# A layer-normalized attention and mixer kernel: the first chunk's q and k made in two halves, and the second chunk turned behind the values

## The chip, the cores and the metric

The kernel runs on one core of one Trainium2 chip. The metric is the device time of one execution in microseconds, taken as the median of several runs. A core has TensorE (PE in the profile; PEld is its weight load), VectorE (DVE), ScalarE (ACT), GpSimd (POOL) and SyncE (SP, which here issues the DMAs). Each engine works through a queue of its own.

## The reference

Cut to what matters, for 2048 rows of 512 numbers:

```python
xn = layernorm(x)                              # over the 512 columns
q, k, v = xn @ wqkv                            # 32 heads of 16 columns
scores = q k^T / 4, row i sees columns i-255 .. i
s = softmax(scores) v @ wo
y = layernorm(xn)
g = silu(gelu(y @ w1 + b1) @ w2 + b2)          # 512 -> 1792 -> 512
out = x + s * g
```

All of it is float32. The kernel reaches that precision with float32r products in three passes: each operand is split into a high part (a cast to float32r) and a low part (the rest), and high times high, high times low and low times high are added up.

## The kernel before

**Chunks and tiles.** The rows are worked on in four chunks of 512 rows, each of four tiles of 128 rows. A chunk is loaded (`xs[c]`), normalized in place, turned by PE (16 transposes of 128x128, four for each of the four 128-column parts `kt`) and split into `big[:, 0, kt]` (high, a cast by ACT) and `big[:, 1, kt]` (low, a subtraction by DVE from the PSUM bank). In the profile `big` is called xnT. Then come its q, k (`job_qk(n, c)`, twelve products of 512 columns, for a group `n` of heads) and its values (`job_v(hf, i)`, 24 products of 256 columns for a pair of 128-row blocks; the tile is pv, or vt after the copy to SBUF).

**Normalization.** `layernorm` (L87) returns the steps of each tile. Either DVE takes the mean and variance (`each`: bn, mvs, ve), POOL takes the power -1/2 (rss), DVE makes the shift, and ACT or DVE applies it (`end`); or, for the tiles named in `by_sums`, ACT takes the sum (`total`), POOL the mean (nm), ACT the squares (`squares`), POOL ve and rss, and `end_sums` the rest. `n_act` is the number of tiles that ACT applies.

**The first chunk.** L762 to L775: for each of the four tiles statistics, normalization and `transpose0`, which writes 128 columns of each of four PSUM tiles `tr0[kt]` (two are called tr in the profile, two fb; each is one bank of 512 columns). Two extra products of `ident` follow the first two tiles. Then ACT casts the weights of q, k (wqb from wqkr), POOL makes their low part, DVE casts the weights of the values (wva from wvr), POOL makes their low part, and L790 splits the four banks, a whole bank at a time.

**The order of the work.** Except for SyncE ahead of L756, a wrapper (`Ordered`) keeps the instructions of each engine in the order of the code. The main loop (L906) runs over slots `t` from -16 on, each of two halves, `fill_in(t, 0)` and `fill_in(t, 1)`. `group(c)` (L795) is a list of jobs that `spread` (L525) lays evenly over eight half slots; for `c = 0` these are slots -16 to -13. At the end of each slot stands `run(lns.get(t))`, further steps of the normalization:

```python
lns = {-16: [ln1[1][1], ln1[0][2], invert3, ln1[2][1], ln1[1][2], ln1[3][1]], -15: [ln2[1][0], ones],
       -14: [ln2[0][0], ln2[2][0], ln2[0][1], ln2[3][0]], -13: [ln2[i][-1] for i in range(4)],
```

`ln1`, `ln2`, `ln3` are the steps of chunks 1, 2, 3; `ones` is a POOL memset of a column of vt. Before, `job_x(1)` (the 16 transposes of chunk 1, each followed in the fourth by ACT's cast and DVE's subtraction) is issued in slot -14, between the two halves of the values `job_v(0, 1)`. Its first three `kt` use the tiles fb0, fb1 and the first bank of zo. `job_qk(0, 1)` in slot -12 writes fb0. The product of `job_qk(0, 0)` lies in the first bank of xy; its high part (sh) is copied by ACT in slot -16, its low part (pjr) is made by DVE in slot -15, and both are sent by DMA to `slots[0]` (qk), from which the first scores, `max_block(0, m)`, are made at the end of slot -12 and later.

**Waits.** The kernel is written in a tile framework: it says which tile each instruction reads and writes, and the framework places the semaphore waits between engines. Where the kernel wants more of them, it adds them by hand (`add_manual_dep`).

Of the kernel before, what the change touches and what calls it, by code (L numbers as in the profile page):

```python
# [9 lines left out]
F32 = mybir.dt.float32  # L10
# [3 lines left out]
ALU = mybir.AluOpType  # L14
# [36 lines left out]
def mixer_kernel(ctx, tc, x, wqk, wv, wo, w1, b1, w2, b2, out):  # L51
# [32 lines left out]
    rss = small.tile([P, 8 * NCH], F32, tag="rs", name="rss", bufs=1)  # L84
    squared = set()

    def layernorm(ts, c, n_act=4, by_sums=(), end_act=False, apart=()):  # L87

        n = len(ts)
        nm = small.tile([P, n], F32, tag="nm", name=f"nm{c}") if by_sums else None  # L90
        sh = small.tile([P, n], F32, tag="shift", name=f"shift{c}")
        mv, sm, rs = mvs[:, n * c: n * c + n], sums[:, n * c: n * c + n], rss[:, n * c: n * c + n]
        squared.update(n * c + i for i in by_sums)

        def total(i):

            nc.scalar.activation(x23[:, 8], ts[i], AF.Identity, accum_out=sm[:, i, 0:1])
            nc.gpsimd.tensor_scalar(nm[:, i: i + 1], sm[:, i, 0:1], -1.0 / D, None, op0=ALU.mult)

        def squares(i):  # L100

            nc.scalar.activation(x23[:, 8], ts[i], AF.Square, bias=nm[:, i: i + 1], accum_out=sm[:, i, 1:2])
            ve = small.tile([P, 1], F32, tag="ve1", name=f"ve{c}_{i}")
            nc.gpsimd.tensor_scalar(ve, sm[:, i, 1:2], 1.0 / D, EPS, op0=ALU.mult, op1=ALU.add)
            nc.gpsimd.tensor_tensor(rs[:, i: i + 1], ve, mhalf[:, :1], op=ALU.pow)

        def end_sums(i):
            if end_act:
                nc.vector.tensor_mul(sh[:, i: i + 1], nm[:, i: i + 1], rs[:, i: i + 1])
                apply(i, True)  # L110
                return
            nc.gpsimd.tensor_scalar(ts[i], ts[i], nm[:, i: i + 1], rs[:, i: i + 1], op0=ALU.add, op1=ALU.mult)

        def each(i):

            st = small.tile([P, 6], F32, tag="bn", name=f"bn{c}_{i}")
            nc.vector.bn_stats(st, ts[i])
            nc.vector.bn_aggr(mv[:, i], st)
            ve = small.tile([P, 1], F32, tag="ve1", name=f"ve{c}_{i}")
            nc.vector.tensor_scalar(ve, mv[:, i, 1:2], EPS, None, op0=ALU.add)  # L120
            if i in apart:
                return lambda: power(i, ve)
            power(i, ve)

        def power(i, ve):
            nc.gpsimd.tensor_tensor(rs[:, i: i + 1], ve, mhalf[:, :1], op=ALU.pow)

        def apply(i, on_act):
            if on_act:
                nc.scalar.activation(ts[i], ts[i], AF.Identity, bias=sh[:, i: i + 1], scale=rs[:, i: i + 1])  # L130
            else:
                nc.vector.tensor_scalar(ts[i], ts[i], mv[:, i, 0:1], rs[:, i: i + 1],
                                        op0=ALU.subtract, op1=ALU.mult)

        def end(i):

            if i < n_act:
                nc.vector.scalar_tensor_tensor(sh[:, i: i + 1], mv[:, i, 0:1], -1.0, rs[:, i: i + 1],
                                               op0=ALU.mult, op1=ALU.mult)
            apply(i, i < n_act)  # L140
        return [(lambda i=i: total(i), lambda i=i: squares(i), lambda i=i: end_sums(i)) if i in by_sums else
                (lambda i=i: each(i), lambda i=i: end(i)) for i in range(n)]

    def run(steps):
        for step in steps:
            step()
# [149 lines left out]
    def job_qk(n, c):  # L296

        box = []
        ops = [(kt, a, b) for kt in range(KT) for a, b in PASSES]
        if not n:  # L300
            ops.sort(key=lambda o: o[2])
        sl = slice(512 * c, 512 * (c + 1))

        def mm(i):
            if i == 0:
                box.append(fill_bank() if c else xy[:, 0])
            kt, a, b = ops[i]
            nc.tensor.matmul(box[0], wqs[n][:, a, kt], big[:, b, kt, sl],
                             start=(i == 0), stop=(i == len(ops) - 1))

        def half(bank, j, i, r, **flags):
            kt, a, b = ops[i]
            return nc.tensor.matmul(bank[:, 0:256], wqs[n][r, a, kt],
                                    big[r, b, kt, 512 * c + 256 * j: 512 * c + 256 * (j + 1)], **flags)

        def send(src, qk, tt):
            copy_rows(slots[n % 2][tt:P:4, qk, :, sl], src[64 * qk: 64 * qk + 64])

        def finish():
            hi = sgp.tile([P, 512], F32R, tag="sh", name=f"sh_{n}_{c}", bufs=2)  # L320
            raw = t2.tile([P, 512], F32, tag="t2", name=f"pjr_{n}_{c}")
            lo = raw.bitcast(F32R)
            if n or c > 1:
                for j, bank in enumerate(box):
                    nc.scalar.copy(raw[:, 256 * j: 256 * (j + 1)], bank[:, 0:256])
                box[:] = [raw]
            wide = 512 // len(box)
            parts = [(bank[:, 0:wide], slice(wide * j, wide * (j + 1))) for j, bank in enumerate(box)]

            def high():  # L330
                for src, at_ in parts:
                    nc.scalar.copy(hi[:, at_], src)
                behind(now[0], send_high)

            def send_high():
                for qk, tt in ((1, 0), (0, 0), (1, 2), (0, 1)):
                    send(hi, qk, tt)

            def low():
                for src, at_ in parts:  # L340
                    (nc.gpsimd if n or c > 1 else nc.vector).tensor_tensor(lo[:, at_], src, hi[:, at_].bitcast(F32),
                                                                  op=ALU.subtract)
                behind(now[0], send_low)

            def send_low():
                send(lo, 1, 1)
                send(lo, 0, 2)

            later(1 if n else 0, high)
            later(3 if n else 1, low)  # L350
        if n or c > 1:
            return half, finish, box
        return [(216, mm, i) for i in range(len(ops))], finish

    def by_halves(job, banks, first, second, seer=None):
# [23 lines left out]
    def job_v(hf, i):  # L379
# [3 lines left out]
        def mm(k):  # L383
            if k == 0:
                box.append(ps_st.tile([P, 2, 256], F32, tag="b", name=f"pv_{hf}_{i}"))
            j, kt, (a, b) = k // 12, k % 12 // 3, PASSES[k % 3]
            kb = 2 * i + j
            nc.tensor.matmul(box[0][:, j], big[:, a, kt, P * kb: P * (kb + 1)], wva[:, b, kt],
                             start=(k % 12 == 0), stop=(k % 12 == 11))
# [372 lines left out]
    def transpose0(i):  # L762
        for kt in range(KT):
            nc.tensor.transpose(tr0[kt][:, P * i: P * (i + 1)], xs[0][i][:, P * kt: P * (kt + 1)], ident)
        for _ in range(2 if i < 2 else 0):
            nc.tensor.matmul(zo[:, 0, 0:P], ident, ident, start=True, stop=True)

    ln = layernorm(xs[0], 0, 3)
    for i in range(4):
        ln[i][0]()  # L770
        if i:
            ln[i - 1][1]()
            transpose0(i - 1)
    ln[3][1]()
    transpose0(3)  # L775
    split_wqk(0)
    ln1 = layernorm(xs[1], 1, 2, by_sums=(0, 1), end_act=True, apart=(3,))
    ln2 = layernorm(xs[2], 2, by_sums=(0,))
    ln3 = layernorm(xs[3], 3, by_sums=range(4))
    n, raw = raws["qk"]  # L780
    nc.gpsimd.tensor_tensor(wqs[0][:, 1], raw, wqs[0][:, 0].bitcast(F32), op=ALU.subtract)
    for j, raw in enumerate(raws["v"]):
        nc.vector.tensor_copy(wva[:, 0, 2 * j: 2 * j + 2], raw)
        nc.gpsimd.tensor_tensor(wva[:, 1, 2 * j: 2 * j + 2], raw, wva[:, 0, 2 * j: 2 * j + 2].bitcast(F32),
                                op=ALU.subtract)
        if j == 0:
            ln1[0][0]()
    nc.gpsimd.affine_select(out=upper, in_=upper, pattern=[[1, P]], compare_op=ALU.is_gt,
                            fill=0.0, base=0, channel_multiplier=-1)
    for kt in range(KT):  # L790
        split(big[:, 0, kt, 0:512], big[:, 1, kt, 0:512], tr0[kt])
    run([ln1[0][1], ln1[1][0], ln1[2][0]])
    invert3 = ln1[3][0]()

    def group(c):  # L795
        if c == 0:
            (ops, finish), (x_ops, _) = job_v(0, 1), job_x(1)
            return [job_qk(0, 0), job_v(0, 0), (ops[:12] + x_ops, lambda: None), (ops[12:], finish)]
        return [job_qk(0, c), job_v(0, 2 * c), job_x(c + 1), job_v(0, 2 * c + 1)]
    for c in range(2):  # L800
        fills.update(spread(group(c), [(4 * c - 16 + i // 2, i % 2) for i in range(8)]))
# [620 lines left out]
```

## Time and profile before

| | |
|---|---|
| median of 3 runs | 733.74 us (733.71 to 734.0) |
| profiled execution | 733.78 us |
| its span in the trace | 732.0 us |
| PE busy | 719.5 us (98%) |
| DVE, ACT, POOL busy | 496.5, 427.7, 321.6 us |
| first product of `job_qk(0, 0)` | 10.76 us from the span's start |
| end of `job_qk(0, 1)` | 24.42 us |

The page of a profile gives busy time by engine over the whole span, and a line of 40 slices. For a change in the first 25 us it is read together with the timeline (each row: start, duration, engine, line, operation, tile written, tile read, shape, count, and in brackets the idle time of the engine just before and what ended it), with the chain that ended last (start, duration, what) and with the table of busy time by stretch. Nearly all instructions carry line L43, that of a helper, so tiles tell them apart. Times are in us from the start of the span.

### The profile page before, as it was taken

Reading aid. Unit: us, or ns where it says so; the run is one execution under the profiler, and the core shown is the slowest. Engines: PE = TensorE matmul, PEld = TensorE weight load, DVE = VectorE, ACT = ScalarE, POOL = GpSimd, SP = SyncE. Lnnn points to the kernel's source line nnn. Section 1 sums busy time; section 2 is a strip of 40 time slices with the busy share of each in tenths; the row PEclk is TensorE's granted clock in tenths of the full one; section 3 lists DMA queues with packets and bytes.
Section 4 is the critical chain, followed back from the end, with each engine's and each line's share of the span. In section 5 each row is a group of like instructions: output and inputs, shape, how many; then the busy total and the mean of one; then the engine's idle time right before and its main releaser. Section 6 shows DMA issues by size and latency. Waiting matters only on the chain.

```text
span 732.0 us, 19063 instructions
## 1 busy us (share of the span) xinstructions
PE 719.5 (98%) x7584; PEld 586.1 (80%) x7584; DVE 496.5 (68%) x735; ACT 427.7 (58%) x724; POOL 321.6 (44%) x678
## 2 busy tenths in 40 slices
PE   8999999999999999999999999999999999999997
PEld 7997777777778887777776788888888888888886
DVE  6887776877766777777882657446687855667823
ACT  7767777877777676888878735232343734541001
POOL 7344767767677665777877540203302000001102
PEclk9999999999999999999999999999999999999999
DMA  8324356777776733667624367347223312253701
GB/s 294 81 48 105 89 137 171 215 229 217 207 197 184 211 119 98 169 160 203 182 79 160 119 230 200 145 130 244 87 57 116 115 59 87 65 189 110 252 19 58
DMA packets 61528, 106.77 MB, mean 146 GB/s; under 512 B 12096, under 2 KB 12352, under 8 KB 61440
## 3 DMA queue, kind: packets, MB, share of 16 engines
q1 hardware_dynamic: 61440, 105.56, 49.3%
q8 instruction: 60, 0.98, 0.6%
q14 instruction: 28, 0.23, 0.1%
HBM read 54.53 MB, written 33.82 MB: 121 GB/s over the span
## 4 chain that ended last, share of the span: by engine, by line
PE 92%; ACT 3%; DVE 2%; DMA 1%; issue 1%; POOL 0%; SPq 0%; DVEq 0%; ACTq 0%; POOLq 0%
PE acc L43 20%; PE fb L43 20%; PE zo L43 13%; PE stb L43 9%; PE p L43 9%; PE s L43 6%; PE h L43 6%; PE xy L43 5%; ACT pt L43 3%; PE pv L43 2%; DMA qk<-pjr 1%; DVE xy L43 0%; DMA x<-in_x_dram 0%; DVE bn L43 0%; DVE mt L43 0%
## 5 line engine op out<-in xcount | busy, mean ns | idle before, releaser
L43 POOL TENSOR_SCALAR_AFFINE_SELECT pt<-pt 128x256 f32<-128x256 f32 x480 | 192.9, 426 | 98.9 <-ACT pt L43 92.2
L43 ACT ACTIVATE pt<-stb 128x768 f32<-128x768 f32 (+1 forms) x244 | 188.7, 773 | 44.7 <-PE stb L43 38.4
L43 DVE TENSOR_REDUCE mt<-xy 128x4 f32<-128x1024 f32 (+1 forms) x128 | 152.6, 1192 | 4.4
L43 DVE COPY_PREDICATED xy<-upper,zo 128x512 f32<-128x512 int32 x112 | 77.8, 695 | 73.3 <-PE xy L43 65.1
L43 POOL TENSOR_TENSOR xo<-xo,gated 128x512 f32<-128x512 f32 x15 | 19.9, 1329 | 221.8 <-DVE gated L43 220.8
L43 PE MATMUL zo<-pt,vt 128*17 128x128 f32 x2880 | 103.7, 275 | 0.0
L43 PE MATMUL stb<-qk 64*128 64x384 f32 (+1 forms) x488 | 94.9, 383 | 4.9 <-ACT pt L43 3.5
L43 PE MATMUL fb<-xnT,wqb 64*128 64x512 f32 (+2 forms) x732 | 99.5, 381 | 0.1
L43 PE MATMUL acc<-w,gh 128*128 128x512 f32 x320 | 98.5, 389 | 0.0
L43 PEld LDWEIGHTS stb<-qk 64*128 64x128 f32 x488 | 45.6, 183 | 48.5 <-ACT pt L43 39.9
L43 PEld LDWEIGHTS zo<-pt,vt 128*17 128x17 f32 x2880 | 67.5, 97 | 15.2 <-issue 5.1
L43 PEld LDWEIGHTS acc<-w,gh 128*128 128x128 f32 x320 | 60.1, 188 | 12.5
L43 PEld LDWEIGHTS fb<-xnT,wqb 64*128 64x128 f32 (+1 forms) x732 | 62.6, 185 | 6.8 <-ACT vt L43 0.4
L43 PE MATMUL acc<-w,gl 128*128 128x512 f32 x160 | 62.4, 390 | 0.2 <-DVE gl L43 0.2
L43 PE MATMUL xy<-qk 64*128 64x256 f32 (+2 forms) x536 | 58.2, 290 | 0.6 <-DVE mt L43 0.6
L43 PE MATMUL p<-xnT 128*128 128x512 f32 x189 | 51.8, 389 | 0.0
L43 PEld LDWEIGHTS xy<-qk 64*128 64x128 f32 x536 | 46.6, 185 | 5.6 <-issue 2.4
L43 ACT COPY oraw<-zo 128x128 f32<-128x128 f32 x108 | 28.7, 266 | 37.0 <-PE zo L43 27.3
L43 ACT ACTIVATE gated<-acc 128x512 f32<-128x512 f32 x16 | 8.7, 596 | 62.4 <-DVE acc L43 62.4
L43 PE MATMUL s<-wos,ohl 128*128 128x512 f32 (+1 forms) x204 | 44.3, 376 | 0.0
L43 PEld LDWEIGHTS s<-wos,ohl 128*128 128x128 f32 x204 | 36.8, 188 | 7.1
L43 PEld LDWEIGHTS p<-xnT 128*128 128x128 f32 x189 | 35.5, 188 | 7.4
(202 smaller groups left out, 1192.9 us busy)
## 6 DMA issues: line engine op xcount, KB each, us to landing
qk<-sh SPq DMA_DIRECT2D x128, 128.0 KB
qk<-pjr SPq DMA_DIRECT2D x64, 128.0 KB
oT_d<-oraw SPq DMA_DIRECT2D x32, 256.0 KB
w_d<-in_w_dram SPq DMA_DIRECT2D x14, 512.0 KB
xt_d<-xnT SPq DMA_DIRECT2D x12, 512.0 KB
x<-in_x_dram SPq DMA_DIRECT2D x16, 256.0 KB
w<-w_d SPq DMA_DIRECT2D x16, 256.0 KB
or<-oT_d SPq DMA_DIRECT2D x16, 256.0 KB
```

Of the source, the lines that this page charges most:

```text
L43: r = issue(*args, **kwargs)
```

## The change

The first chunk's q, k are made in two halves of 256 columns. ACT casts the first half of each bank (`cast0(0)`, from the first two tiles) before the third tile is transposed into it, the second half (`cast0(1)`) after the fourth; DVE subtracts by halves (`rest0`). The products of `job_qk(0, 0)` become 24 of 256 columns, and their passes are in another order, as are those of `job_v(0, 0)`. The shifts of chunk 0 are made by POOL, the q, k weights are cast by DVE, and ACT takes the second half of the cast of the values' weights. The first sum of chunk 1 goes behind these casts, and `job_x(1)` behind all of `job_v(0, 1)`, into slot -13. `lns` stays as it is.

```diff
-    def layernorm(ts, c, n_act=4, by_sums=(), end_act=False, apart=()):
+    def layernorm(ts, c, n_act=4, by_sums=(), end_act=False, apart=(), shift_apart=False):
...
-            if i < n_act:
+            if i < n_act and shift_apart:
+                nc.gpsimd.tensor_scalar(sh[:, i: i + 1], mv[:, i, 0:1], rs[:, i: i + 1], -1.0, op0=ALU.mult, op1=ALU.mult)
+            elif i < n_act:
                 nc.vector.scalar_tensor_tensor(sh[:, i: i + 1], mv[:, i, 0:1], -1.0, rs[:, i: i + 1],
...
+        def mm_first(k):
+            if k == 0:
+                box.append(xy[:, 0])
+            j, i = k // 12, k % 12
+            parts = ((0, 0), (0, 1), (1, 0)) if j == 0 else ((0, 0), (1, 0), (0, 1))
+            kt, (a, b) = i % KT, parts[i // KT]
+            cols = slice(256 * j, 256 * (j + 1))
+            nc.tensor.matmul(box[0][:, cols], wqs[n][:, a, kt], big[:, b, kt, cols], start=(i == 0), stop=(i == 11))
...
+        if c == 0:
+            return [(109, mm_first, k) for k in range(24)], finish
...
             j, kt, (a, b) = k // 12, k % 12 // 3, PASSES[k % 3]
+            if i == 0:
+                kt, (a, b) = k % KT, ((0, 0), (1, 0), (0, 1))[k % 12 // KT]
...
+    def cast0(half):
+        for kt in range(KT):
+            cols = slice(256 * half, 256 * half + 256)
+            nc.scalar.copy(big[:, 0, kt, cols], tr0[kt][:, cols])
+
+    def rest0(half):
+        for kt in range(KT):
+            cols = slice(256 * half, 256 * half + 256)
+            nc.vector.tensor_sub(big[:, 1, kt, cols], tr0[kt][:, cols], big[:, 0, kt, cols].bitcast(F32))
+
+    ln = layernorm(xs[0], 0, 3, shift_apart=True)
     for i in range(4):
         ln[i][0]()
-        if i:
-            ln[i - 1][1]()
-            transpose0(i - 1)
-    ln[3][1]()
-    transpose0(3)
-    split_wqk(0)
+        if i == 3:
+            n, raw = raws["qk"]
+            wqs[0] = bigp.tile([P, 2, KT, P], F32R, tag="wb0", name="wqb0")
+            nc.vector.tensor_copy(wqs[0][:, 0], raw)
+        ln[i][1]()
+        if i == 2:
+            cast0(0)
+        transpose0(i)
+    nc.gpsimd.tensor_tensor(wqs[0][:, 1], raw, wqs[0][:, 0].bitcast(F32), op=ALU.subtract)
+    cast0(1)
+    rest0(0)
+    for j, raw in enumerate(raws["v"]):
+        (nc.scalar.copy if j else nc.vector.tensor_copy)(wva[:, 0, 2 * j: 2 * j + 2], raw)
+        nc.gpsimd.tensor_tensor(wva[:, 1, 2 * j: 2 * j + 2], raw, wva[:, 0, 2 * j: 2 * j + 2].bitcast(F32),
+                                op=ALU.subtract)
+    rest0(1)
...
-    n, raw = raws["qk"]
-    nc.gpsimd.tensor_tensor(wqs[0][:, 1], raw, wqs[0][:, 0].bitcast(F32), op=ALU.subtract)
-    for j, raw in enumerate(raws["v"]):
-        nc.vector.tensor_copy(wva[:, 0, 2 * j: 2 * j + 2], raw)
-        nc.gpsimd.tensor_tensor(wva[:, 1, 2 * j: 2 * j + 2], raw, wva[:, 0, 2 * j: 2 * j + 2].bitcast(F32),
-                                op=ALU.subtract)
-        if j == 0:
-            ln1[0][0]()
...
-    for kt in range(KT):
-        split(big[:, 0, kt, 0:512], big[:, 1, kt, 0:512], tr0[kt])
-    run([ln1[0][1], ln1[1][0], ln1[2][0]])
+    run([ln1[0][0], ln1[1][0], ln1[0][1], ln1[2][0]])
...
         if c == 0:
-            (ops, finish), (x_ops, _) = job_v(0, 1), job_x(1)
-            return [job_qk(0, 0), job_v(0, 0), (ops[:12] + x_ops, lambda: None), (ops[12:], finish)]
+            return [job_qk(0, 0), job_v(0, 0), job_v(0, 1), job_x(1)]
```

More of the change, by code (lines that the diff above doesn't have):

```diff
@@ L766, in transpose0 @@
             nc.tensor.matmul(zo[:, 0, 0:P], ident, ident, start=True, stop=True)
-    ln = layernorm(xs[0], 0, 3)
+    def cast0(half):
[7 more added lines that the diff above has]
+    ln = layernorm(xs[0], 0, 3, shift_apart=True)
     for i in range(4):
         ln[i][0]()
-        if i:
-            ln[i - 1][1]()
-            transpose0(i - 1)
-    ln[3][1]()
-    transpose0(3)
-    split_wqk(0)
+        if i == 3:
[14 more added lines that the diff above has]
+    rest0(1)
     ln1 = layernorm(xs[1], 1, 2, by_sums=(0, 1), end_act=True, apart=(3,))
```

## The prediction

> **What bounds the kernel now.** I read the page first, for the share of each engine and the clock. TensorE (PE) is the kernel's bound.
>
> ```profile
> span 732.0 us, 19063 instructions
> PE 719.5 (98%) x7584; PEld 586.1 (80%) x7584; DVE 496.5 (68%) x735; ACT 427.7 (58%) x724; POOL 321.6 (44%) x678
> PEclk9999999999999999999999999999999999999999
> ```
>
> The profiled execution took 733.78 us against its span of 732.0 and the median of 733.74; I sum against 733.78, which is the median within 0.04. The change touches only the first 25 us, so the busy time by stretch comes next.
>
> ```profile
> core 0: us, PE busy (x) PEld busy (x) DVE busy (x) ACT busy (x) POOL busy (x), PEclk, DMA share, GB/s
> 10.70:14.05 3.35, 3.29 (x14) 2.52 (x15) 3.26 (x6) 2.65 (x7) 3.27 (x5) 1.00 1.06 407
> 14.05:18.36 4.31, 4.31 (x37) 4.18 (x36) 2.54 (x9) 3.20 (x8) 3.04 (x9) 1.00 0.83 244
> 18.36:24.42 6.06, 6.06 (x42) 5.28 (x41) 5.77 (x16) 4.40 (x10) 2.15 (x6) 1.00 0.30 67
> 24.42:40.00 15.58, 15.55 (x178) 14.58 (x178) 12.85 (x22) 11.91 (x27) 7.54 (x18) 1.00 0.31 70
> ```
>
> From the first real product on, PE hasn't 0.1 us to give in 30 us. Whatever moves the end of a product in this stretch moves the end of the kernel by as much, and nothing behind it can give time back. The chain that ended last says which products these are:
>
> ```profile
> 10.76 3.28 PE xy L43 x12
> 14.05 4.31 PE pv L43 x36
> 18.36 1.00 PE fb L43 x8
> 19.36 0.44 PE zo L43 x4
> 19.80 0.44 PE tr L43 x4
> 20.24 1.44 PE pv L43 x12
> 21.67 2.75 PE fb L43 x12
> 24.42 0.37 PE xy L43 x4
> ```
>
> In words: q, k of chunk 0 (xy), 36 products of the values (pv), 16 transposes of chunk 1 (fb, zo, tr: 1.88 us), 12 more pv, q, k of chunk 1 (fb), then the first scores. The 12 pv behind the transposes fill the time in which ScalarE (ACT) casts and VectorE (DVE) subtracts what was transposed. My yardstick is the end of q, k of chunk 1: 24.42 before. There are two questions: when the values start (14.05 before), and whether chunk 1's casts are ready when PE gets there.
>
> **Part by part: the first chunk in halves.** GpSimd (POOL) now makes the shifts.
>
> ```profile
> 6.96 0.15 DVE L43 TENSOR_SCALAR ve<-mvs 128x1 f32<-128x1 f32 x1
> 7.19 0.55 POOL L43 TENSOR_TENSOR rss<-ve,mhalf 128x1 f32<-128x1 f32 x1 [0.51 <-DVE shift L43]
> 8.29 0.81 ACT L43 ACTIVATE x<-x,shift,rss 128x512 f32<-128x512 f32 x1 [0.26 <-DVE shift L43]
> 9.01 0.60 ACT L43 CAST wqb<-wqkr 128x512 fp32r<-128x512 f32 x1
> 12.54 0.26 POOL L43 TENSOR_SCALAR nm<-sums 128x1 f32<-128x1 f32 x1
> ```
>
> The third tile's variance is ready 0.07 earlier (one DVE shift less ahead of it), at 7.04; power 7.12 to 7.67; a POOL shift like the nm row, 0.22 to 0.26, ends at 7.96; ACT normalizes that tile from 8.00 instead of 8.29, and takes its next instruction 0.72 later (8.29 to 9.01), at 8.72. That 0.29 is the gain of the shifts. The weights' cast leaves ACT for DVE, where a 128x512 cast takes 0.38 (two in 0.75, quoted below) between the variance and the last tile's normalization; it delays nothing, since GpSimd's power for that tile takes 0.55 meanwhile.
>
> Now four casts of 256 columns from PSUM, then four DVE subtractions of 256:
>
> ```profile
> 39.75 0.65 ACT L43 COPY pjr<-fb 128x256 f32<-128x256 f32 x2 [1.11 <-PE fb L43]
> L43 ACT COPY pjr<-fb 128x256 f32<-128x256 f32 x4 | 1.3, 376 | 1.1 <-PE fb L43 1.1
> L43 DVE TENSOR_TENSOR gated<-s,gated 128x256 f32<-128x256 f32 x2 | 0.8, 425 | 1.2 <-PE s L43 1.2
> DVE xy L43 <- ACT oraw L43: 0.9, 2, 0.7
> ```
>
> A cast is 0.38 and the next starts 0.27 after it: 8.72 to 9.91. The last row decides how the halves meet. That DVE instruction reads columns 0 to 255 of zo, ACT's oraw copy reads columns 256 to 383 of zo's second bank, yet the one waits for the other: the framework that places the waits orders engines by bank, disjoint columns or not, reads too. So the third tile's transposes, written into the banks that are being cast, wait for these casts: the fourth starts at 9.95, the last tile's (0.11 each by the chain's rows) at 10.06, the second half's casts at about 10.5, and the first half's subtraction, which reads a bank that ACT is then reading for the second half, at about 10.9. Four at some 0.36 (0.425 less an overlap of 0.06) end at 12.4. Before, PE's first product came at 10.76; now it comes at about 10.4, but after four products it stands before weights-high times x-low, the second group of the first half, until 12.4. From there 17 products of 0.12 (36 pv in 4.31) end at 14.49: the values start 0.44 later than before. [...]
>
> **The values' weights and the second chunk's normalization.** They hang on the same subtractions, by queue order.
>
> ```profile
> 9.32 0.75 DVE L43 CAST wva<-wvr 128x512 fp32r<-128x512 f32 x2
> 12.77 1.30 POOL L43 TENSOR_TENSOR wva<-wvr,wva 128x512 fp32r<-128x512 f32 x1
> 14.02 0.29 POOL L43 TENSOR_SCALAR_AFFINE_SELECT upper<-upper 128x128 f32<-128x128 f32 x1
> 12.84 0.73 ACT L43 ACTIVATE x<-x,nm 128x512 f32<-128x512 f32 x1 [0.67 <-POOL nm L43]
> 15.46 0.73 ACT L43 ACTIVATE x<-x,nm 128x512 f32<-128x512 f32 x1 [0.58 <-POOL nm L43]
> 17.78 0.55 DVE L43 TENSOR_SCALAR x<-x,mvs,rss 128x512 f32<-128x512 f32 x1 [0.36 <-POOL rss L43]
> 18.24 0.68 DVE L43 TENSOR_TENSOR pjr<-xy,sh 128x512 fp32r<-128x512 f32 x1
> ```
>
> DVE casts half of wva at 12.35 to 12.73 (before: 9.32). POOL subtracts two halves, 1.25 each (12.77 to 14.02), to 15.27; both low halves are ready for the products that use them, since those now come last in the first pair of values (from 15.45 on). But POOL's queue holds the mask (0.29) and then chunk 1's first mean, nm, behind them: nm ends at 15.82, where it ended at 12.80. ACT's squares(0) starts at 15.86 instead of 12.84, the copy sh (0.57, as the vt row below) follows, and squares(1) starts at about 17.13 instead of 15.46. From there the rows of before go on: 2.32 to DVE's last normalization (15.46 to 17.78), so 19.45 to 20.0. PE's 48 values run from 14.49 to 20.24 (0.12 each), so the transposes of chunk 1 don't wait: the 12 values put ahead of them just cover 1.7 us of lateness. They end at 22.12.
>
> **The second chunk's casts.** Here is the cost. Chunk 1's transposes were issued at slot -14 and are now at -13, while the statistics of chunk 2 stay at the end of slots -15 and -14. Those of slot -14 (the first tile's sum and squares on ACT, nm on POOL) stood behind the casts in their queues; now they are ahead.
>
> ```profile
> 18.84 0.68 DVE L43 BATCH_NORM_STATS2 bn<-x 128x6 f32<-128x512 f32 x1
> 19.84 1.28 DVE L43 TENSOR_TENSOR xnT<-fb,xnT 128x512 fp32r<-128x512 f32 x2
> 20.00 0.55 POOL L43 TENSOR_TENSOR rss<-ve,mhalf 128x1 f32<-128x1 f32 x1 [2.26 <-DVE ve L43]
> 20.50 0.58 POOL L43 MEMSET vt<- 128x256 f32 x1
> 21.72 0.22 POOL L43 TENSOR_SCALAR nm<-sums 128x1 f32<-128x1 f32 x1 [0.64 <-ACT x L43]
> 18.96 1.07 ACT L43 CAST xnT<-fb 128x512 fp32r<-128x512 f32 x2 [0.16 <-PE fb L43]
> 21.98 0.73 ACT L43 ACTIVATE x<-x,nm 128x512 f32<-128x512 f32 x1 [0.35 <-POOL nm L43]
> 22.70 0.57 ACT L43 COPY vt<-pv 128x512 f32<-128x512 f32 x1
> ```
>
> The new chain, step by step: pjr on DVE 0.46 after the last normalization (17.78 to 18.24), 19.91; POOL's power for chunk 2's second tile 1.76 behind pjr (18.24 to 20.00), 21.67; the memset 22.17 to 22.75; only then POOL's nm for chunk 2's first tile, whose sum ACT has had since about 21.6; ACT's squares 0.26 after nm's start (21.72 to 21.98), 23.01; the next ACT instruction 0.72 later (21.98 to 22.70), 23.73. That is now chunk 1's first cast, which stood at 18.96. It ends at 24.30, DVE's subtraction (0.68, as pjr) at 25.02; DVE's three statistics (1.00 each, 18.84 to 19.84) are done by 23.5 and don't count. The q, k product of chunk 1 takes the bank of the first transposes (fb0), so it can't start before that subtraction: 25.06, where PE has been free since 22.12. Later casts come every 0.53 and keep ahead of its 2.75 us: it ends at 27.81. Against 24.42 that is +3.39 us: 733.78 + 3.39 = 737.2.
>
> Behind that point PE finds its inputs no later in relation than before: chunk 2's statistics are done, and the sends of chunk 0's q, k leave at about 17 and 20.6, over 7 us ahead of the scores that read them. SP's queue keeps its order. So the whole 3.4 us stays.
>
> **The rivals.** (a) *Not slower: chunk 1's casts are not held up.* [...] It decides if chunk 2's nm runs 3 us earlier than I have it. For it: ACT's sum is there in time. Against it: every engine is held to the order of the code, and the trace shows it; at 21.98 ACT stood 0.35 for nm while the vt copy behind it, whose product ended at 21.67, waited until 22.70.
>
> (b) *Halves released by columns.* [...] The waits row speaks against it.
>
> (c) *PE's clock falls in the gap.* PE stands still about 3.0 us after 1.88 us of transposes; PEclk never left 9 before, but the rows hold no such gap behind 10.76. At half rate the 12 products would take 5.5 instead of 2.75, so up to +2.75 more: 737.2 to 739.9, and I take 738.9 for a fall that lasts part of that stretch and of the next. [...]
>
> **How the numbers follow.** Forecast 0.70, own range 736.4 to 738.0: the 256-wide DVE step (0.36 to 0.43, four on the chain), the POOL subtractions (1.25 to 1.30) and the order of POOL's four powers move it by some tenths each. Rival (a) 0.07, (b) 0.08, (c) 0.15. The range 735.5 to 739.0 leaves out (a), some of (b) and the far end of (c). What can be told from no change is about 0.2%, 1.47 us, that is 735.2 and 732.3: the forecast, (c) and most of (b) are slower by more, 0.88; (a) and the rest of (b) are within, 0.09; 0.03 is left for faster, which no case of mine gives.
>
> **What would show it.** In the changed profile: the third tile's transposes behind ACT's 256-wide casts; a PE wait of over 1 us between the first and second group of q, k of chunk 0; values from about 14.5; and, above all, a PE gap of about 3 us ahead of chunk 1's fb products, put down to DVE xnT, with ACT's squares and POOL's memset and nm between the transposes and the first cast. I am wrong if values start by 13 or if that gap is under 1.5 us.

## The result, and the profile after

The changed kernel takes 739.43 us (median of 6 runs, 738.27 to 739.86); the kernel before, 733.87 us (6 runs, 733.52 to 734.09). The ratio is 1.0073, interval 1.0063 to 1.0084: slower by 5.56 us, 2.17 more than the forecast's 3.39 and 0.43 above its range. The profiled execution took 739.86 with a span of 738.1; it is the slowest of the six, so the rows below are those of a run 0.43 above the median.

The page of the changed kernel, the lines that answer to those of before, and one group:

```profile
span 738.1 us, 19099 instructions
PE 722.2 (98%) x7596; PEld 588.1 (80%) x7596; DVE 498.6 (68%) x736; ACT 427.8 (58%) x728; POOL 321.8 (44%) x681
PEclk9999999999999999999999999999999999999999
L43 PE MATMUL fb<-xnT,wqb 64*128 64x512 f32 (+2 forms) x732 | 101.2, 384 | 3.0 <-DVE xnT L43 2.9
```

PE's share is still 98%, and every slice of the clock still reads 9: a slice is 18 us wide, too coarse for what happened. But the group of the q, k products has a wait of 2.9 us in one piece, for DVE's xnT. That is the announced gap. Busy time by stretch of the changed kernel, cut at PE's own marks:

```profile
core 0: us, PE busy (x) PEld busy (x) DVE busy (x) ACT busy (x) POOL busy (x), PEclk, DMA share, GB/s
10.91:14.87 3.96, 3.84 (x27) 3.20 (x26) 3.60 (x10) 3.01 (x9) 1.77 (x2) 1.00 1.06 407
14.87:20.63 5.76, 5.76 (x50) 5.76 (x49) 2.88 (x11) 3.72 (x8) 4.05 (x10) 1.00 0.50 136
20.63:25.43 4.80, 1.92 (x18) 1.68 (x17) 4.03 (x12) 3.53 (x9) 2.75 (x7) 1.00 0.38 85
25.43:30.04 4.61, 4.61 (x14) 3.45 (x14) 1.95 (x6) 2.91 (x5) 0.94 (x2) 0.63 0.00 0
30.04:45.00 14.96, 14.93 (x167) 13.95 (x168) 12.65 (x19) 9.54 (x23) 5.15 (x14) 1.00 0.31 73
```

The rows are q, k of chunk 0 in halves; all 48 values; the transposes of chunk 1 (1.92 of PE's time) and the gap; q, k of chunk 1; the scores and what follows. Two things are new. PE stands still for 2.88 of the 4.80 us ahead of the second q, k. And these products then run at a granted clock of 0.63 and take 4.61 instead of 2.75 (before, 21.67 to 24.42). Their end, my yardstick, is 30.04 instead of 24.42: +5.62. Afterwards PE is full again at 1.00 and gives nothing back. The last products (s) end at 734.40 instead of 728.31, +6.09; the other 0.47 of this one execution comes somewhere between 45 and 465 us, and its cause is not shown.

The chain that ended last (start, duration, what) now leaves PE in this stretch:

```profile
13.10 2.55 POOL wva L43 x2
15.65 0.24 POOL upper L43
15.90 0.24 POOL nm L43
16.16 0.82 ACT x L43 x2
...
19.96 0.55 DVE x L43
20.51 0.60 DVE pjr L43
...
22.19 0.55 POOL rss L43
22.74 0.50 POOL vt L43
23.24 0.11 POOL nm L43
...
24.18 0.48 ACT xnT L43
24.68 0.70 DVE xnT L43
...
25.43 4.61 PE fb L43 x12
```

It reads as the prediction has it: POOL's two subtractions for wva, the mask, chunk 1's mean, ACT's squares, chunk 1's last normalization, pjr, POOL's power, its memset (vt), chunk 2's mean, the first cast, the subtraction. Each piece stands 0.30 to 0.52 later than forecast. Where these tenths came from is seen on DVE and POOL, in the timeline:

```profile
8.90 1.26 POOL L43 TENSOR_TENSOR wqb<-wqkr,wqb 128x512 fp32r<-128x512 f32 x1
8.96 1.48 DVE L43 TENSOR_SCALAR x<-x,mvs,rss 128x512 f32<-128x512 f32 x1 [0.44 <-POOL rss L43]
10.50 0.44 PE L43 MATMUL tr<-ident,x 128*128 128x128 f32 x2
11.27 0.76 DVE L43 TENSOR_TENSOR xnT<-tr,xnT 128x256 fp32r<-128x256 f32 x2 [0.82 <-ACT xnT L43]
14.87 5.92 PE L43 MATMUL pv<-wva,xnT 128*128 128x256 f32 x48
```

DVE's normalization of the last tile, 0.55 before, takes 1.48 here and ends at 10.44, 0.28 after POOL's subtraction (10.16). The tile's transposes start at 10.50 (forecast 10.06), the first subtraction at 11.27 (10.9), the values at 14.87 (14.49). The normalization and the subtraction stand side by side from 8.96 to 10.16; in the experiment below that starts POOL's subtraction later, at 9.89, the normalization takes 0.55 again.

So the +5.62 are, in this trace: 3.39 as forecast, 0.37 for a first stage that is later than forecast, most of it by the disturbed normalization, and 1.86 (4.61 less 2.75) for the products behind the gap. Of this 1.6 are the clock's, since the same products take 3.02 behind a gap at full clock (next section); the other 0.27 come with the gap alone.

### The profile page after: what moved, and what is told of

Its sections match the earlier page's. It is cut to its first block, busy times and chain, and to the rows that moved or that the text cites. A ratio compares the mean times of both kernels' runs of the same rounds, so it can differ in the third digit from the quotient of the medians.

```text
span 738.1 us, 19099 instructions
## 1 busy us (share of the span) xinstructions
PE 722.2 (98%) x7596; PEld 588.1 (80%) x7596; DVE 498.6 (68%) x736; ACT 427.8 (58%) x728; POOL 321.8 (44%) x681
## 4 chain that ended last, share of the span: by engine, by line
PE 90%; ACT 3%; DVE 2%; POOL 2%; issue 1%; DMA 1%; SPq 0%; DVEq 0%; ACTq 0%; POOLq 0%
PE fb L43 20%; PE acc L43 20%; PE zo L43 13%; PE p L43 9%; PE stb L43 9%; PE s L43 6%; PE h L43 6%; PE xy L43 5%; ACT pt L43 2%; DMA qk<-pjr 1%; PE pv L43 1%; POOL rss L43 1%; DVE xy L43 0%; DMA x<-in_x_dram 0%; DVE xnT L43 0%
## 5 line engine op out<-in xcount | busy, mean ns | idle before, releaser
L43 PE MATMUL fb<-xnT,wqb 64*128 64x512 f32 (+2 forms) x732 | 101.2, 384 | 3.0 <-DVE xnT L43 2.9
```

Of the source, the lines that this page charges most:

```text
L43: r = issue(*args, **kwargs)
```

## The experiments

My theory after this: the jobs' order alone, x(1) behind all values while chunk 2's statistics stay where they are, makes a gap of about 2 us; the late halves widen it to 2.9; a gap of that length makes PE's clock fall in some runs. Rivals: the slow products are due to their operands and not to the gap; the gap is due to the halves alone.

**PE kept busy in the gap.** Eight products of ident, which nothing reads, are added behind chunk 1's transposes.

```diff
     fills[-10, 0][:0] = fills[-11, 1][-5:]
+    def keep_busy():
+        for _ in range(8):
+            nc.tensor.matmul(xy[:, 1, 0:P], ident, ident, start=True, stop=True)
+    fills[-13, 1].append((keep_busy, ()))
```

> The changed kernel with 8 extra products of the identity on PE (into the second bank of xy, which nothing reads) behind chunk 1's transposes, inside the gap of 2.9 us. Theory (the clock fell in the gap): the 12 fb products take 2.75 us again instead of 4.61, the clock row of 24 to 32 us is 1.00, about 737.6 us. Rival (the fb products were slow because their inputs came late): they stay at 4.6, 739.4.

737.70 us (737.58 to 737.83, 4 runs), ratio to before 1.0053 (1.0038 to 1.0068). The timeline of PE, where each product of ident is two records:

```profile
22.12 1.95 PE L43 MATMUL xy<-ident 128*128 128x128 f32 x16
25.18 3.02 PE L43 MATMUL fb<-xnT,wqb 128*128 128x512 f32 x12 [1.10 <-DVE xnT L43]
```

The products take 3.02 in this view, where the changed kernel's row is 4.61, and the granted clock of the four runs is 0.999 to 1.000. More work on PE, and 1.7 us less time: the slow products are due to the gap, not to their operands or to a bank, which are the same here. What is left, 3.96 us over before (737.70 less 733.74, the kernel before on the same chip), stands beside 3.39 + 0.37 + 0.27 = 4.03 for the late products without the clock.

**Chunk 2's statistics behind chunk 1's casts.**

```diff
-    lns = {-16: ..., -15: [ln2[1][0], ones],
-           -14: [ln2[0][0], ln2[2][0], ln2[0][1], ln2[3][0]], -13: [ln2[i][-1] for i in range(4)],
+    lns = {-16: ..., -15: [],
+           -14: [], -13: [ln2[1][0], ones, ln2[0][0], ln2[2][0], ln2[0][1], ln2[3][0]] + [ln2[i][-1] for i in range(4)],
```

> The changed kernel with chunk 2's statistics (slots -15 and -14) moved behind chunk 1's transposes and casts, to the end of slot -13. Theory (the statistics ahead of the casts make the gap): no PE gap of over 0.3 us ahead of fb, fb from about 22.7 to 25.5, no slower clock, about 734.9 us. Rival (the casts are late because chunk 1's normalization and pjr are late): a gap of over 1.5 us remains, 737 us or more.

737.89 (736.96 to 738.79, 4 runs), ratio 1.0056 (1.0041 to 1.0071). PE and DVE in the timeline:

```profile
22.74 3.02 PE L43 MATMUL fb<-xnT,wqb 128*128 128x512 f32 x12 [0.19 <-DVE xnT L43]
30.64 0.66 PE L43 MATMUL xy<-qk 64*128 64x256 f32 x4 [1.93 <-DVE mt L43]
29.89 0.69 DVE L43 TENSOR_REDUCE mt<-xy 128x4 f32<-128x512 f32 x1
```

The gap goes (2.89 to 0.19) and the products start at 22.74 instead of 25.43: the statistics ahead of the casts were its cause. My time was a miss, because they cannot stand behind the casts free of charge: DVE's three sets now lie ahead of the first maxima (mt), and PE waits 1.93 us for mt 8 us later. Two of the four runs (738.79 and 738.46) have a mean clock of 0.998; the first is the profiled one, and there the clock is at 0.50 from 30.82 to 34.23, behind that wait. The other two, 736.96 and 737.33, show no fall.

**The old order of the jobs in the changed kernel, and the new order alone in the kernel before.** These two take the change apart.

```diff
-            return [job_qk(0, 0), job_v(0, 0), job_v(0, 1), job_x(1)]
+            (ops, finish), (x_ops, _) = job_v(0, 1), job_x(1)
+            return [job_qk(0, 0), job_v(0, 0), (ops[:12] + x_ops, lambda: None), (ops[12:], finish)]
```

> The changed kernel with the order of jobs of before (chunk 1's transposes between the two halves of the second pair of values). Theory (chunk 1's normalization, at 20.5 us, is late by way of the halves): PE waits about 1.2 us at the transposes, the 12 values behind them cover the casts, fb ends at about 26.7, 736.1 us, full clock. Rival (only the new order costs): no wait, fb ends at about 25.2, 734.6 us.

736.21 (735.92 to 736.92, 5 runs), ratio 1.0034 (1.0021 to 1.0048). The halves without the new order cost 2.5 us (736.21 less 733.74): chunk 1 is normalized too late for the earlier transposes, and there is no gap ahead of fb:

```profile
20.89 0.98 PE L43 MATMUL fb<-ident,x 128*128 128x128 f32 x7 [1.11 <-ACT x L43]
24.02 2.91 PE L43 MATMUL fb<-xnT,wqb 128*128 128x512 f32 x12
```

The reverse of this diff, in the kernel before:

> The kernel before with only the new order of jobs (transposes of chunk 1 behind all values). Theory (the order alone puts statistics ahead of the casts): a PE gap of about 1.8 us ahead of fb, fb ends at about 26.3, 735.6 us if the clock stays, up to 737.3 if it falls. Rival (the order is harmless without the halves): 733.9 us.

735.91 (7 runs), ratio 1.0036 (1.0025 to 1.0048): five runs of 735.64 to 736.02 at a mean clock of 0.999 or 1.000, and two of 737.42 and 737.46 at 0.998. The order alone costs 2.2 us, and in two runs of seven 1.5 more. PE in its trace, one of the five:

```profile
23.25 3.01 PE L43 MATMUL fb<-xnT,wqb 128*128 128x512 f32 x12 [1.91 <-DVE xnT L43]
```

Either part is slower by itself, by a little over 2 us, through different waits; the sum is 4.6. Together, without the clock, they cost 4.0 with PE kept busy, and 4.4 and 4.7 in the two runs of the changed kernel that show no fall (738.27 and 738.60, less 733.87). That is about the sum: as built here, neither part has a gain that the other spoils.

**The q, k weights' cast behind the last normalization.** It makes POOL's subtraction start after DVE's normalization.

```diff
-        if i == 3:
...
-            nc.vector.tensor_copy(wqs[0][:, 0], raw)
         ln[i][1]()
+        if i == 3:
...
+            nc.vector.tensor_copy(wqs[0][:, 0], raw)
```

> The changed kernel with DVE's cast of the q, k weights behind its normalization of the last tile, so that POOL's subtraction of these weights no longer runs beside that normalization. Theory (the two engines disturb each other: 1.48 us beside POOL, 0.55 alone): the normalization takes about 0.55 and ends by 9.5, the last tile's transposes start at about 10.1 instead of 10.50, the values at about 14.45 instead of 14.87. Rival (1.48 has another cause): it stays over 1.2 us and nothing moves earlier.

740.74, one run, mean clock 0.995. DVE, POOL and PE in the timeline, then a stretch as above:

```profile
8.93 0.55 DVE L43 TENSOR_SCALAR x<-x,mvs,rss 128x512 f32<-128x512 f32 x1 [0.67 <-POOL rss L43]
9.89 1.28 POOL L43 TENSOR_TENSOR wqb<-wqkr,wqb 128x512 fp32r<-128x512 f32 x1 [1.00 <-DVE wqb L43]
14.65 5.92 PE L43 MATMUL pv<-wva,xnT 128*128 128x256 f32 x48
25.21 5.49 PE L43 MATMUL fb<-xnT,wqb 128*128 128x512 f32 x12 [2.89 <-DVE xnT L43]
```

```profile
25.21:30.70 5.49, 5.49 (x14) 3.87 (x14) 1.94 (x6) 2.90 (x5) 0.93 (x2) 0.50 0.00 0
```

The normalization is back at 0.55, so POOL's subtraction beside it was what stretched it. The values start 0.22 earlier than in the changed kernel, about half of the 0.42 that I expected. The first tile's statistics start 0.54 earlier in this run (3.46 and 4.00), but the third tile's then wait 0.52 for its load, and from there the two runs are level: the third tile is on ACT at 8.21 and 8.14, the last normalization starts at 8.93 and 8.96. So 0.2 to 0.3 us are the normalization's. The time is worse because the clock fell for longer: the stretch has a granted clock of 0.50 over all 5.49 us: half speed, and twice the 2.75 of before.

**The second halves in banks of their own.** The diff writes tiles 3 and 4 to `xy[:, 1]` and `zo[:, 0]` instead of to the banks that are being cast.

```diff
+    def at0(half, kt):
+        return (xy[:, 1] if kt < 2 else zo[:, 0])[:, 256 * (kt % 2): 256 * (kt % 2 + 1)] if half else tr0[kt][:, 0:256]
```

> The changed kernel with the second halves (tiles 3 and 4) turned into other banks, the second bank of xy and the first of zo, so that a half shares no bank with the other half of its part. Theory (waits go by bank): the third tile's transposes start at about 9.0 without waiting for ACT's casts, DVE's first subtraction follows the last normalization at 10.5 instead of 11.27, values from about 14.1 instead of 14.87, everything behind 0.7 to 0.8 us earlier. Rival (the columns were released before already): the same times as in the changed kernel.

739.73, one run, mean clock 0.998: a miss. DVE and PE:

```profile
10.32 0.74 DVE L43 TENSOR_TENSOR xnT<-tr,xnT 128x256 fp32r<-128x256 f32 x2
11.97 0.74 DVE L43 TENSOR_TENSOR xnT<-xy,xnT 128x256 fp32r<-128x256 f32 x2
12.87 4.36 PE L43 MATMUL xy<-xnT,wqb 128*128 128x256 f32 x24 [1.76 <-DVE xnT L43]
```

The first half's subtraction no longer waits for the second half's casts (10.32, right behind the normalization, instead of 11.27). But the first q, k product, which writes the first bank of xy, waits until 12.87 for DVE's subtraction that reads xy's second bank (11.97 to 12.71). The order is kept by tile: xy is one tile of two banks. The clock falls behind this wait (0.50 from 12.32 to 15.73), and not behind the later one of 1.90 us ahead of fb.

**The same in zo's two banks only**, with the extra products of the start moved to xy and the memset of otb behind the halves:

```diff
-        return (xy[:, 1] if kt < 2 else zo[:, 0])[:, 256 * (kt % 2): 256 * (kt % 2 + 1)] if half else tr0[kt][:, 0:256]
+        return zo[:, kt // 2][:, 256 * (kt % 2): 256 * (kt % 2 + 1)] if half else tr0[kt][:, 0:256]
```

> The changed kernel with the second halves turned into the two banks of zo (parts 0, 1 in the first, 2, 3 in the second), a tile that neither the first halves nor the product of q, k uses. Theory (waits go by tile, and the halves of one tile held each other): no PE wait for ACT's casts at the third tile, DVE's first subtraction right behind its last normalization, the first q, k product not held back as it was by xy's readers, values from about 14.1 instead of 14.87. Rival (what held the halves was DVE's work alone): values from 14.7 or later.

737.22, one run, clock 1.000.

```profile
8.71 1.48 DVE L43 TENSOR_SCALAR x<-x,mvs,rss 128x512 f32<-128x512 f32 x1 [0.44 <-POOL rss L43]
10.66 3.37 PE L43 MATMUL xy<-xnT,wqb 128*128 128x256 f32 x24
13.87 5.91 PE L43 MATMUL pv<-wva,xnT 128*128 128x256 f32 x48
24.27 3.02 PE L43 MATMUL fb<-xnT,wqb 128*128 128x512 f32 x12 [2.74 <-DVE xnT L43]
```

The products run through and the values start at 13.87; in the kernel with PE kept busy, whose normalization starts within 0.02 of this one (8.69), they start at 14.62. So the tiles that both halves share cost the first stage 0.75. The gap behind it stays (2.74), without a fall of the clock in this run.

**Chunk 1's first sum ahead of the second half.**

```diff
+    ln1 = layernorm(xs[1], 1, 2, by_sums=(0, 1), end_act=True, apart=(3,))
+    ln1[0][0]()
     cast0(1)
     rest0(0)
...
-    run([ln1[0][0], ln1[1][0], ln1[0][1], ln1[2][0]])
+    run([ln1[1][0], ln1[0][1], ln1[2][0]])
```

> The changed kernel with the first sum of chunk 1 on ACT and its mean on POOL ahead of the second half's casts and of the values' weights. Theory (chunk 1 is late because nm stands behind the weights' subtractions in POOL's queue): squares(0) at about 13 instead of 16.16, squares(1) at about 16.2 instead of 17.35, chunk 1 normalized by about 19.3 instead of 20.5, chunk 1's first cast at about 23 instead of 24.09, a PE gap of about 1.8 instead of 2.89. Rival (it is late by way of DVE): less than 0.4 us of that.

736.78, one run, clock 0.999.

```profile
24.36 3.02 PE L43 MATMUL fb<-xnT,wqb 128*128 128x512 f32 x12 [2.02 <-DVE xnT L43]
```

With POOL's first mean ahead of its subtractions the gap shrinks from 2.89 to 2.02, that of the new order alone (1.91). That is the step of the halves in the gap, POOL's queue, shown by itself; the other 2 us belong to the order.

**All mends together.** Banks of xy and zo, weights' cast late, sum early, the mask's affine_select moved from its place ahead of chunk 1's statistics to slot -15, and the old order of the jobs:

> The halves kept, what held them taken away: second halves in other banks, weights' cast behind the last normalization, chunk 1's first sum early, both sums ahead of the squares, the mask in slot -15, and the order of jobs of before. Theory: values from about 13.3 instead of 14.05 in the kernel before, chunk 1 normalized by about 17.4, no PE gap and no fall of the clock, q, k of chunk 1 ends about 0.7 us earlier than in the kernel before, 733.0 us. Rival (the second chunk's normalization gives it back): 733.8 us or more, with a PE wait at the transposes of chunk 1.

736.76 (735.09 to 737.5, 6 runs), ratio 1.0040 (1.0027 to 1.0052). A miss, for the same reason as with two banks: the first q, k product waits 2.09 us, until 12.04. The profile puts the end of this wait down to ACT's wva, but DVE's reads of xy's other bank end at 11.89, as long before the product as in the two-bank experiment (0.15 and 0.16), and with zo's banks, below, the wait is gone. The clock adds to it: five of the six runs have a mean of 0.997 or 0.998 (736.65 to 737.5), the sixth 1.000 (735.09), and in the profiled run it is at 0.50 from 12.58 to 16.00. With zo's banks instead:

> The version meant to be best, with the second halves in zo instead of xy: halves apart, weights' cast behind the last normalization, chunk 1's sums early, mask late, order of jobs of before. Theory: values from about 13.3 (14.05 in the kernel before), chunk 1 normalized by about 17.4, no PE gap, full clock, 733.0 us. Rival (chunk 1's normalization gives it back): a PE wait of 0.5 us or more at its transposes, 733.6 us or more.

733.24 (732.69 to 733.85, 10 runs) against 733.74 of before (27 runs), ratio 0.9993, interval 0.9984 to 1.0003.

```profile
13.29 4.48 PE L43 MATMUL pv<-wva,xnT 128*128 128x256 f32 x36
20.78 2.91 PE L43 MATMUL fb<-xnT,wqb 128*128 128x512 f32 x12
```

PE has no gap ahead of fb and the clock is 0.999 or 1.000 in all ten runs: together the mends, the old order of the jobs among them, take back all of the 5.6 us; what each of them brings beside the others is not shown. The medians are 0.5 us apart in its favour, but the interval holds 1: it is no proven gain over the kernel before.

**The small parts alone in the kernel before.** Shifts by POOL, the weights' cast by DVE and another order of the passes (the diff shows the first two):

```diff
-    ln = layernorm(xs[0], 0, 3)
+    ln = layernorm(xs[0], 0, 3, shift_apart=True)
...
-    split_wqk(0)
+    nc.vector.tensor_copy(wqs[0][:, 0], raw)
```

> The kernel before, no halves, old order of jobs: POOL makes chunk 0's shifts, DVE casts the q, k weights behind the last normalization, and the products of q, k take the low weights second. Theory (ACT's queue of that moment holds the first cast): the first product at about 10.5 instead of 10.76, 733.4 us. Rival (the gain is eaten by the second chunk's normalization): 733.7 us, with a PE wait of 0.2 to 0.3 us at chunk 1's transposes.

735.15 (734.22 to 736.14, 11 runs), ratio 1.0019 (1.0010 to 1.0028): a miss. Five of the runs have a mean clock of 0.996 to 0.998 (735.74 to 736.14), the other six 0.999 or 1.000 (734.22 to 735.15). In the profiled run, one of these five, PE waits 2.34 us for the first tile from ACT, and the clock is at 0.50 from 8.16 to 11.57. And the shifts alone:

> The kernel before with POOL making chunk 0's shifts and nothing else. Theory (ACT normalizes the third tile 0.15 us earlier): the first product 0.1 to 0.15 us earlier, 733.6 us. Rival (POOL's queue is later for it and the last tile's power with it): 733.7 to 733.9 us.

734.25 (733.75 to 735.41, 11 runs), ratio 1.0010 (1.0002 to 1.0019): a miss too, with three runs at a mean clock of 0.997 or 0.998 (734.99 to 735.24). POOL and ACT:

```profile
5.71 0.56 POOL L43 TENSOR_TENSOR rss<-ve,mhalf 128x1 f32<-128x1 f32 x1 [0.44 <-DVE ve L43]
6.38 0.26 POOL L43 TENSOR_SCALAR shift<-mvs,rss 128x1 f32<-128x1 f32 x1
6.67 1.71 ACT L43 ACTIVATE x<-x,shift,rss 128x512 f32<-128x512 f32 x2 [1.84 <-POOL shift L43]
```

The kernel before issues the statistics of tile i ahead of the end of tile i-1. On DVE that costs the first shift 0.27 (power until 5.68, shift from 5.95); on POOL the first tile's shift (6.38) stands behind the second tile's power (5.71), and ACT starts 3.15 after the first bn (3.52), where before it started 2.21 after it (3.93 to 6.14). The changed kernel issues each tile's end right behind its statistics, and there the shifts bring most of what I forecast: the third tile is on ACT 4.14 after the first bn instead of 4.36, 0.22 of 0.29. So the shift's gain hangs on the loop's order, which I had not said.

## Why the prediction was right and wrong

**Right: the sign and the mechanism.** The chain of the forecast is the chain of the trace, piece by piece: third tile on ACT at 8.14 (8.00), q, k held up by the first half's low parts, POOL's subtractions with the mask and the mean behind them, chunk 1 normalized at 20.51 (20.0), the power and the memset ahead of chunk 2's mean, the first cast at 24.09 (23.73), the products at 25.43 (25.06). The rivals (a) and (b), not slower or halves released by columns, did not happen: values at 14.87 are on the far side of 13, a gap of 2.89 on the far side of 1.5. No run shows the values by 13, which was an estimate: with the halves in zo's two banks they start at 13.87, with all mends and zo's banks at 13.29. One sign did not show in the form that I gave: there is no PE wait of over 1 us inside q, k of chunk 0. The four products of the second group start at 11.75, 12.08, 12.41 and 12.74, one behind each subtraction, and the profile counts PE as busy between them; at 0.12 each, the last would have started 0.9 earlier.

**Wrong, first: the case that I did not choose.** The step that failed is the price of the 12 products behind the gap: the sum has them at full clock, 2.75, and gives the other case, rival (c), 0.15. They took 4.61. The clock did fall: in four of the six runs the mean is 0.997 or 0.998 (739.41 to 739.86), and in the two without a fall the time is 738.27 and 738.60. No row of before tested a gap of 3 us, as the prediction says itself, so nothing stood behind so small a chance. With the fall, the sum is 733.87 + 3.39 + 0.37 + 1.86 = 739.49, beside a median of 739.43. That closeness is partly luck: without the fall (3.02 for the products) the same sum gives 737.9, and the two runs without one are 0.4 and 0.7 above it, which stays open. The size for (c), +1.7 to 738.9, was close to the 1.86; what lifted it over the range is the next point.

**Wrong, second: DVE's last normalization.** I let it take 0.55, as before, where it had stood alone, and did not put POOL's subtraction for the q, k weights beside it. The change moves that subtraction from 9.69 to 8.90, onto it. It took 1.48, but most of this is covered, since the last tile's transposes come behind the third's anyway. With the weights' cast late they start 0.44 behind the third's last row (9.88 and 10.32); here that would have been 10.25, and it was 10.50. So 0.25 of the 0.37 by which everything is later are the normalization's, as an estimate from these rows, and 0.12 the third tile's, which came 0.14 later than forecast. (The sum itself has 0.05 too much: 17 products of 0.12 from 12.4 end at 14.44, not 14.49. No reading hangs on it.)

**By tile, not by bank.** The prediction read the order of DVE's xy behind ACT's oraw as an order by bank. The wait in the two-bank experiment goes over both banks of a tile: the product that writes xy's first bank starts at 12.87, 0.16 after the subtraction that reads the second ends (12.71). For tr and fb, one bank each, the two give the same, so the forecast is not touched. That row, which I took for an order by bank, agrees with both and does not tell the two apart.

## What to carry to other kernels

A step moved later in one queue must be checked against everything that stays put beside it: here the transposes moved one slot, the next chunk's statistics did not, and that alone cost 2.2 us of 5.6. Price a gap that you open on PE twice, once as idle time and once as the clock that may fall behind it: here gaps of 1.8 us and more had falls in a part of their runs, one of 2.9 in most, and a fall cost 1.6 (4.61 less 3.02). Fill such a gap, or put the fall into the sum. When work moves from one of DVE and POOL to the other, look at what the other is doing in the same microsecond (here a normalization of 0.55 took 1.48), and at the order in which the loop issues it.

## What the runs showed of the hardware

*The clock.* Up to 40 us of these traces a fall of the clock to 0.50 lasts 3.41 us (25.48 to 28.89 in the changed kernel), or twice that with the weights' cast late (24.48 to 31.30), and the stretches at full clock between the clock's first record and a fall are whole multiples of 3.41 us (20.48, six times, in the changed kernel). So the traces are cut here into windows of that length, counted from the fall or the first record. Three of them, each the one that lies over the wait: the changed kernel and the statistics behind, where the fall follows at the window's end, and the early sum, where none follows. The second figure of a row is PE's busy time, the third from the end the granted clock:

```profile
22.07:25.48 3.41, 0.52 (x6) 0.29 (x4) 2.71 (x9) 2.14 (x6) 2.80 (x7) 1.00 0.33 77
27.41:30.82 3.41, 1.48 (x13) 1.28 (x14) 2.05 (x7) 2.96 (x6) 2.03 (x4) 1.00 0.00 0
20.72:24.13 3.41, 1.62 (x15) 1.38 (x13) 2.67 (x9) 2.96 (x8) 2.54 (x7) 1.00 0.33 77
```

From the first record to 40 us there are six falls in the 14 profiles. The window ahead of each has PE busy for 0.52, 1.07, 1.24, 1.32, 1.36 or 1.48 us; all others have 1.62 or more (1.62 twice, 1.69, 2.0 and up), and no fall follows them. So the limit lay somewhere between 1.48 and 1.62 of 3.41 us here. That the runs of one kernel differ by how the windows happen to lie over its gap is my estimate, since each kernel has one trace. (With the weights' cast late, PE was busy for 2.68 us of the window from 24.48 to 27.89, at 0.50, and the next window stayed at 0.50.) The gap of 2.89 lay nearly whole in one window; that of 2.74 with zo's banks was parted between two, which had 2.45 and 1.62 of work. An estimate from this, with windows that start at random: a window takes in the 1.8 to 1.9 us of idle time that a fall needs in seven to eight runs of ten for a gap of 2.89, in at most five of ten for 1.91, and never for 1.10. By time and mean clock the falls were 4 of 6, 2 of 7 and 0 of 4.

The window ahead of the fall with the statistics behind held 1.48 us of products. In the window of the early sum PE did nothing but these float32 transposes, for 1.62 us, and the clock stayed at 1.00.

*DVE beside POOL.* A 128x512 normalization took 1.48 when it began 0.06 after a POOL subtraction of 1.26 (changed kernel, 8.96 and 8.90), and 0.55 when the subtraction came later (weights' cast late, 8.93 and 9.89). In the first case it ended 0.28 after the subtraction.
